# Signs of the weights from GpSimd, and two instructions instead of three for a weight block on VectorE

## The chip, the cores and the metric

The kernel runs on one core of one Trainium2 chip. The metric is device time in microseconds (us). The engines of the core are TensorE (PE; its weight loads are listed as PEld), VectorE (DVE), ScalarE (ACT), GpSimd (POOL) and SyncE (SP), which issues most of the DMAs. Each engine takes its instructions in the order in which they were written and waits on semaphores for the others.

## The reference

```python
q_n, k_n = rmsnorm(q, g_q), rmsnorm(k, g_k)         # q, k, v: 8 x 12 heads x 448 x 64, float32
attn = softmax(q_n @ k_n.T / sqrt(64))              # per head
x = (attn @ v) as 3584 tokens x 768
h = maximum(maximum(x @ w1, x @ w2), x @ w3)        # four weights of 768 x 768
out = h @ w_out                                     # float32, 3584 x 768
```

The four weights come out of the setup as 64-bit floats, two 32-bit words each. [...]

## The kernel before

**The order of the work.** The 96 heads are taken as 48 pairs, and each pair has 12 beats (`beat(g, i)`, pair g, beat i from 0). A beat issues a fixed list of pieces on all engines; `later(n, work)` puts work n beats on, and `tick()` at the end of a beat issues what is due. Nothing is reordered: the program's order is each engine's order. In a pair, VectorE takes the row maxima of the scores (L702) in beats 2, 5, 8 and 11, ScalarE the exponentials (L718), PE scores, transposes and products with V. At the same time the rows of Q and K of a later pair are prepared: GpSimd squares them (`sq`, L450, behind the row maxima of beats 2 and 5), VectorE sums the squares (`ss`, L457, beats 4 and 7), GpSimd makes the inverse root (`ri`, L467 and L471) and scales the rows (`kn`, `qn`, L479). In the first six pairs (`PLAIN = 6`) attention is done in 32-bit floats; from the seventh on everything is split into two 16-bit parts, and PE also has the two layers of the feed-forward network between (L889, L951).

**Ties.** In the first six pairs `follow()` ties GpSimd to VectorE: VectorE sets one element of `here` (L164), and GpSimd copies it (L165) and so waits until VectorE has come to that place. Before the change the ties lie ahead of the four row maxima of a pair, so that GpSimd's `sq`, `kn` and `qn` run beside them.

**The weights.** There are 24 blocks of 128 x 768 weights: 18 of w1, w2 and w3, then 6 of w_out. A block is loaded by SP into one of three `raw` buffers (768 KB, low and high words alternating, L224 and L229). The first 18 blocks are begun every 4 beats, the rest every 8 (`BLOCK_BEATS`). `prep_block` issues for each: on ScalarE a multiplication of the high words by 2 ** -112, in place (`rebias`, L189), and on VectorE three steps (`decode`), in the second, third and fourth beat after:

```python
f  = upper << 3                        # L197, tensor_scalar
f |= upper & 0x80000000                # L201, scalar_tensor_tensor
f |= lower >> 29                       # L206, scalar_tensor_tensor
```

Here `f` is the block's plain 32-bit form in the tile `w_sb`. The shift by 3 drops the sign bit, which the second step puts back. One beat later the buffer is loaded again. When three blocks are there, PE makes products of them (`marks`, L281), VectorE takes their largest (L169, `most`), GpSimd makes a scale (`w_up`, L300 and L301), and a block is split into two 16-bit parts, on ScalarE (L310) and VectorE (L313), two 128 x 768 operations. `largest_v` finds the largest value of V for a batch, by products on PE (L593) and a maximum on VectorE (L169, `v_rows`), in the later batches by VectorE alone.

Of the kernel before, what the change touches and what calls it, by code (L numbers as in the profile page):

```python
# [9 lines left out]
F32 = mybir.dt.float32  # L10
# [4 lines left out]
ALU = mybir.AluOpType  # L15
# [20 lines left out]
BLOCK_BEATS = (4, 8)  # L36
# [12 lines left out]
def qknorm_attention_maxout_ffn_kernel(  # L49
# [73 lines left out]
    def later(beats, work, last=False):  # L123

        due.setdefault(clock[0] + beats, ([], []))[last].append(work)
# [65 lines left out]
    def decode(raw, f, stage):  # L191

        bits = raw.rearrange("p (n t) -> p n t", t=2)
        upper, lower = bits[:, :, 1], bits[:, :, 0]
        f = f.bitcast(U32)
        if stage == 0:
            nc.vector.tensor_scalar(  # L197
                out=f, in0=upper, scalar1=3, scalar2=None, op0=ALU.logical_shift_left
            )
        elif stage == 1:  # L200
            nc.vector.scalar_tensor_tensor(  # L201
                out=f, in0=upper, scalar=0x80000000, in1=f,
                op0=ALU.bitwise_and, op1=ALU.bitwise_or,
            )
        else:
            nc.vector.scalar_tensor_tensor(  # L206
                out=f, in0=lower, scalar=29, in1=f,
                op0=ALU.logical_shift_right, op1=ALU.bitwise_or,
            )

    blocks = [("in", ft, j) for ft in range(NFT) for j in range(NJ)]
    blocks += [("out", ft, 3) for ft in range(NFT)]
# [22 lines left out]
    def prep_block(n):  # L235
        kind, ft, j = blocks[n]
        raw = raws[n]
        f = plain(w_sb, n) if kind == "in" else plain(wo_sb, ft)
        rebias(raw)

        for stage in range(3):
            later(2 + stage, lambda stage=stage: decode(raw, f, stage), True)
        if kind == "out":
            bound_block(ft, f)
        later(5 if kind == "in" else 9, load_raw)
        if j == NJ - 1:
            later(5, lambda: bound_in(ft), True)
        elif kind == "out" and ft == NFT - 1:
            later(10, bound_out, True)
# [317 lines left out]
    def largest_v(t):  # L567

        b, n = divmod(t, 2)
        if b not in v_rows:  # L570
            v_rows[b] = sb.tile([P, 2], F32, name="v_rows", bufs=2)
        rows = slice(0, P if b else KEYS)
        values = v_tiles[t][rows].rearrange("p h n d -> p (h n d)")
        to = v_rows[b]
        if b >= SQUARED:
            parts = sb.tile([P, 2], F32, name="v_parts", bufs=2)
            half = NP * 2 * D

            def second():
                row_largest(parts[:, 1:2], values[:, half:])  # L580
                nc.vector.tensor_tensor(
                    out=to[:, n:n + 1], in0=parts[:, 0:1], in1=parts[:, 1:2], op=ALU.max
                )

            row_largest(parts[:, 0:1], values[:, :half])
            later(2, second)
            return
        box = ps_m.tile([P, 512], F32, name="marks", tag="m")
        halves = values.bitcast(BF16).rearrange("p (n t) -> p n t", t=2)
        blocks = NP * 4 * D // P  # L590
        for c in range(blocks):
            f = halves[:, c * P:(c + 1) * P, 1]
            nc.tensor.matmul(box[:, 0:P], f, f, start=c == 0, stop=c == blocks - 1)  # L593
        later(1, lambda: row_largest(to[:, n:n + 1], box[:, 0:P]))
# [400 lines left out]

    x_of = [[] for _ in range(B)]
    queue = []
    decoded = [0]

    owed = [0.0]  # L1000

# [92 lines left out]
    def beat(g, i):  # L1094
        w, n = g - 1, g + 2
        c, part = divmod(i, 3)
        k = 4 * g + c
        early = k + 1 <= 4 * PLAIN
        if i == 0 and 0 < g <= PLAIN:
            keep_turned(w, 3)  # L1100
        if part == 0:
            if g < G:
                if k > 4 * PLAIN:
                    row_max(g, c)
                softmax(g, c)
            if early:
                scores(*divmod(k + 1, 4))
            if g < PLAIN:
                if c > 0:
                    turn_plain(g, c - 1)  # L1110
            elif k == 4 * PLAIN:
                pass
            elif 0 < k <= 4 * G:
                lower_weights(*divmod(k - 1, 4))
        if part == 1:
            if c > 0 and g < PLAIN:
                keep_turned(g, c - 1)
            if PLAIN <= g < G:
                upper_weights(g, c)
        if part == 2:  # L1120
            if early:
                if g < PLAIN:
                    follow()
                row_max(*divmod(k + 1, 4))
            elif k + 1 < 4 * G:
                scores(*divmod(k + 1, 4))
        if 0 <= w < PLAIN:
            if i == 1:
                guard_sums(w)
            if i == 2:  # L1130
                inverse_sums(w)
            if i == 5:
                spread_sums(w)
            if i == 6:
                keep_sums(w)
            if i == (8 if w < PLAIN else 9):
                scale_plain(w)
        if w >= 0 and i == (2 if w < PLAIN else 7):
            add_values(w)
        of = THIRDS if g > 2 * NP or (g == 2 * NP and i > 10) else THIRDS_0  # L1140
        thirds(of[i] + (len(queue) > 1 and i % 6 == 4))
        if w >= 0 and i == (9 if 0 < w < PLAIN else 10):
            finish(w, x_of[w // NP])
        if w >= 0 and g % NP == 0 and i == (6 if w < PLAIN else 10):
            queue.append(ffn(w // NP, x_of[w // NP]))

        if g + 1 < G:
            if g + 1 < PLAIN:
                if i in (1, 4):
                    turn_whole(g + 1, "kq"[i // 4])  # L1150
                if i in (2, 5):
                    keep_whole(g + 1, "kq"[i // 5])
            else:
                if i == 0:
                    upper_rows(g + 1, "q")
                if i in (0, 1):
                    lower_rows(g + 1, "kq"[i])
                if i in (2, 3):
                    turn_rows(g + 1, "kq"[i - 2])
                if i == 5:  # L1160
                    swap_keys(g + 1)

        if PLAIN <= n < G and i == 11:
            upper_rows(n, "k")
        if g < PLAIN:
            if i in (2, 5):
                squares(n, "kq"[i // 3])
            if i == 11:
                turn_plain(g, 3)
            if i in (4, 7):  # L1170
                sum_squares(n, "kq"[i // 7])
            if i in (5, 8):
                if i == 8:
                    scale_rows(n, "k")
                inv_rms(n, "kq"[i // 8])
            if i == (9 if n >= PLAIN else 11):
                scale_rows(n, "q")
        elif n < G:
            if i in (0, 3):
                squares(n, "kq"[i // 3])  # L1180
            if i in (2, 5):
                sum_squares(n, "kq"[i // 3])
            if i in (5, 7):
                inv_rms(n, "kq"[i // 7])
            if i in (8, 9):
                scale_rows(n, "kq"[i - 8])

        if g == 0 and i in (0, 3):
            load_v(i // 3)
            later(10 if i == 0 else 11, lambda: largest_v(i // 3))  # L1190
        if g % 3 == 0 and g + 6 < G and i == 9:
            load_v(g // 3 + 2)
            later(8, lambda: largest_v(g // 3 + 2))
        if g == 1 and i == 4:
            bound_v(0)
        if g % NP == NP - 1 and g + 1 < G and i == 7:
            bound_v(g // NP + 1)
        if PLAIN <= g < G and i == 9:
            scale_v(g)
        if PLAIN <= g < G and i == 11:  # L1200
            upper_v(g)
        if PLAIN <= w and i == 0:
            lower_v(w)
        if PLAIN <= w and i == 1:
            shift_values(w)

        if g + 3 < G:
            if i == 0:
                load_k(g + 3)
            if i == 1:  # L1210
                load_q(g + 3)
        if i == 2 and w >= PLAIN:
            turn_weights(w, 3)
        if PLAIN <= g < G and i in (5, 8, 11):
            turn_weights(g, i // 3 - 1)
        n_in = min(decoded[0], NFT * NJ)
        due_at = BLOCK_BEATS[0] * n_in + BLOCK_BEATS[1] * (decoded[0] - n_in)
        if decoded[0] < len(blocks) and clock[0] > due_at:
            later(0, lambda n=decoded[0]: prep_block(n), True)
            decoded[0] += 1  # L1220
        tick()
# [41 lines left out]
```

## Time and profile before

| | |
|---|---|
| Median of 3 runs | 1017.15 us (1016.62 to 1017.98) |
| The profiled execution | 1017.41 us, span 1015.6 us |
| Busy share of the span | PE 96%, VectorE 68%, ScalarE 62%, GpSimd 59% |
| VectorE from 50 to 100 us | 49.70 of 50 us |
| VectorE from 400 to 500 us | 70.90 of 100 us |
| GpSimd from 50 to 100 us | 36.45 of 50 us |
| PE idle up to 250 us | 33 us of 250 |

The span is the time from the first to the last instruction of the profiled execution; the device time includes what lies around it. All rows of the profile come from that one execution. A timeline row gives the start and the length of an instruction in us, the engine, the line, the operation, what it writes and reads, and, in brackets, how long the engine stood idle ahead of it and what ended that. A row of a tile or a line gives the least, the median and the largest length in nanoseconds. An operation may be recorded as beginning a little before the one ahead of it has ended.

### The profile page before, as it was taken

How to read it: one execution, taken by the hardware profiler on the slowest of the kernel's cores; microseconds unless marked ns; L12 is line 12 of the kernel's file. 1: busy time of each engine (PE TensorE's matmuls, PEld its weight loads, DVE VectorE, ACT ScalarE, POOL GpSimd, SP SyncE). 2: the span in 40 equal slices, each digit the busy share in tenths (PEclk: the TensorE clock that was granted, in tenths of full speed). 3: DMA queues.
4: the chain of work that ended last, by engine and by line, in shares of the span. 5: the costliest groups of instructions: out<-in, count | busy, mean ns of one | idle time of the engine just before them, and what ended most of it. 6: DMA issues, size and time to landing. Idle time of an engine off the chain costs nothing.

```text
span 1015.6 us, 17562 instructions
## 1 busy us (share of the span) xinstructions
PE 977.4 (96%) x6045; PEld 527.5 (52%) x6045; DVE 692.9 (68%) x1365; ACT 624.7 (62%) x1419; POOL 602.4 (59%) x683
## 2 busy tenths in 40 slices
PE   8988689889999999999999999999999999999998
PEld 5555345445555555555555555555555555555554
DVE  6899988887767666685767666775767657660120
ACT  6798675667666765666666666657666766651111
POOL 6677875678566666666776666666667757310000
PEclk9999889999999999999999999999999999999999
DMA  9867798989999899998989999999989998751001
GB/s 241 226 174 188 197 179 177 186 149 163 209 165 179 165 204 183 186 166 172 204 155 184 174 206 166 190 159 190 197 162 182 176 186 139 146 92 55 1 1 63
DMA packets 519550, 165.95 MB, mean 163 GB/s; under 512 B 494436, under 2 KB 515236, under 8 KB 519460
## 3 DMA queue, kind: packets, MB, share of 16 engines
q1 hardware_dynamic: 456480, 148.83, 75.5%
q10 hardware_dynamic: 62980, 16.00, 8.6%
q8 instruction: 48, 0.79, 0.3%
q14 instruction: 42, 0.34, 0.1%
HBM read 53.28 MB, written 11.01 MB: 63 GB/s over the span
## 4 chain that ended last, share of the span: by engine, by line
PE 60%; DMA 1%; DVE 0%; ACT 0%; issue 0%; SPq 0%
PE acc L889 34%; PE acc L951 12%; PE av L860 6%; PE sc L680 6%; PE sc L687 1%; DMA pt<-pp 0%; DVE pp L815 0%; DMA out_dram<-osb 0%; ACT osb L960 0%; DVE nm L702 0%; ACT pp L805 0%; ACT qp L499 0%; PE most L604 0%; ACT ht L909 0%; SPq L834 0%
## 5 line engine op out<-in xcount | busy, mean ns | idle before, releaser
L889 PE MATMUL acc<-xt,w_sb 128*128 128x448 f16 x2592 | 516.4, 354 | 0.0
L889 PEld LDWEIGHTS <-w_sb 128*128 128x128 f16 x2592 | 251.4, 98 | 242.3 <-issue 14.0
L718 ACT ACTIVATE sc<-sc,nm 128x448 f32<-128x448 f32 x294 | 178.9, 609 | 187.5 <-DVE nm L702 182.9
L702 DVE TENSOR_REDUCE nm<-sc 128x2 f32<-128x896 f32 x192 | 186.2, 970 | 99.4 <-PE sc L680 58.5
L805 ACT ACTIVATE pp<-sc,rs 128x448 f16<-128x448 f32 x294 | 173.0, 633 | 80.3 <-ACT sc L718 36.4
L815 DVE SCALAR_TENSOR_TENSOR pp<-sc,rs,pp 128x448 f16<-128x448 f32 x294 | 187.9, 675 | 0.9 <-ACT pp L805 0.9
L471 POOL TENSOR_TENSOR ri<-ri,half_neg 128x7 f32<-128x7 f32 x96 | 146.6, 1527 | 8.0
L951 PE MATMUL acc<-w_sb,ht 128*128 128x384 f16 x864 | 148.1, 326 | 1.6 <-ACT osb L960 1.3
L505 POOL TENSOR_TENSOR kp<-kn,kp 128x448 f16<-128x448 f32 x42 | 43.5, 1036 | 157.9 <-ACT kp L499 142.3
L680 PE MATMUL sc<-kt,qt 128*128 128x448 f16 x504 | 116.8, 354 | 10.6 <-DVE pp L815 10.4
L951 PEld LDWEIGHTS <-ht 128*128 128x128 f16 x864 | 83.7, 98 | 61.0 <-issue 5.8
L680 PEld LDWEIGHTS <-qt 128*128 128x128 f16 x504 | 48.8, 98 | 56.4 <-DVE pp L815 10.7
L860 PE MATMUL av<-pt,vp 128*64 128x448 f16 x672 | 72.6, 355 | 0.6 <-DMA pt<-pp 0.6
L918 POOL COPY hx<-ht 128x128 f16<-128x128 f16 x48 | 15.4, 322 | 95.6 <-DVE ht L913 94.9
L875 DVE SCALAR_TENSOR_TENSOR xt<-av,xt 128x448 f16<-128x448 f32 x42 | 26.2, 624 | 62.6 <-ACT xt L874 62.6
L647 POOL TENSOR_TENSOR vp<-vr,vp 128x512 f16<-128x512 f32 x42 | 49.3, 1174 | 21.0 <-ACT vp L641 21.0
L457 DVE TENSOR_REDUCE ss<-sq 128x7 f32<-128x448 f32 x96 | 57.9, 603 | 5.1 <-ACT sq L448 4.3
L505 POOL TENSOR_TENSOR qp<-qn,qp 128x448 f16<-128x448 f32 x42 | 46.3, 1103 | 22.3 <-ACT qp L499 21.4
L903 DVE TENSOR_TENSOR m<-acc,m 128x448 f32<-128x448 f32 x54 | 33.1, 614 | 33.1 <-PE acc L889 33.0
L860 PEld LDWEIGHTS <-vp 128*64 128x64 f16 x672 | 36.0, 109 | 34.7 <-issue 15.8
L488 POOL TENSOR_TENSOR qn<-qn,gain 128x448 f32<-128x448 f32 x42 | 49.0, 1167 | 3.3
L467 POOL TENSOR_SCALAR ri<-ss 128x7 f32<-128x7 f32 x54 | 20.1, 373 | 51.1 <-DVE ss L457 49.9
(140 smaller groups left out, 1159.2 us busy)
## 6 DMA issues: line engine op xcount, KB each, us to landing
raw<-in_moe_w_dram SPq DMA_DIRECT2D x18, 768.0 KB, 5.6
kt<-kt SPq DMA_DIRECT2D x84, 112.0 KB, 2.6
out_dram<-osb SPq DMA_DIRECT2D x24, 384.0 KB, 2.6
vr<-in_v_dram SPq DMA_DIRECT2D x42, 192.0 KB, 4.2
kr<-in_k_dram ACTq DMA_DIRECT2D x34, 224.0 KB, 3.1
qr<-in_q_dram ACTq DMA_DIRECT2D x34, 224.0 KB, 4.4
raw<-in_moe_w_out_dram SPq DMA_DIRECT2D x6, 768.0 KB, 5.0
vs<-vp SPq DMA_DIRECT2D x84, 48.0 KB, 2.5
```

The costliest lines, as they stand in the source:

```text
L457: nc.vector.tensor_reduce(sums[g % 2][:, KQ[what]], sq, axis=AX, op=ALU.add)
L471: nc.gpsimd.tensor_tensor(out=ri, in0=ri, in1=half_neg[:, at], op=ALU.pow)
L505: nc.gpsimd.tensor_tensor(out=parts[:, :, 1], in0=n, in1=parts[:, :, 0], op=ALU.subtract)
L647: nc.gpsimd.tensor_tensor(out=vp[:, 1], in0=values_of(g).rearrange("p h n d -> p (h n) d"), in1=vp[:, 0], op=ALU.subtract,)
L680: nc.tensor.matmul(sc[:, h, :S], qt[:, 4 * h + c], kt[:, n, keys[h]], start=n == 0, stop=n == 1,)
L702: nc.vector.tensor_reduce(nm[:, :n], sc[:, :n, :S], axis=AX, op=ALU.max, negate=True)
L718: nc.scalar.activation(to, sc[:, h, :S], AF.Exp, bias=nm[:, h:h + 1], accum_out=total,)
L805: nc.scalar.activation(pp[:, h, 0], sc[:, h, :S], AF.Copy, scale=rs[:, h:h + 1])
L815: nc.vector.scalar_tensor_tensor(out=pp[:, h, 1], in0=sc[:, h, :S], scalar=rs[:, h:h + 1], in1=pp[:, h, 0], op0=ALU.mult, op1=ALU.subtract,)
L860: nc.tensor.matmul(av[half, :S], values, pt[:, 7 * h + block, SHIFT[h]:SHIFT[h] + S], start=n == 0, stop=n == len(steps) - 1,)
L889: nc.tensor.matmul(acc[:, :S], wt[:, wp, c], xs[c][:, xp], start=(c == 0 and n == 0), stop=(c == NCT - 1 and n == 2),)
L951: nc.tensor.matmul(acc[:, :HW], lhs, wo_sb[:, f, wp, half * HW:(half + 1) * HW], start=(f == 0 and n == 0), stop=(f == NFT - 1 and n == 2),)
```

## The change

GpSimd multiplies the high words of a block, read as 32-bit floats, by 0.0: the result is a zero with the weight's sign, and it is written to the block's place in `w_sb` (the new `sign`). VectorE then needs two steps: `f |= upper << 3`, in one instruction with two inputs, and `f |= lower >> 29`. They come in the second and third beat after `rebias`, and the raw buffer of the first 18 blocks is loaded again one beat earlier. `sign` must read the high words before `rebias` changes them, so it is issued 3, 1 or 2 beats ahead of the block's beginning for the three blocks of a pair (beats 10, 4 and 7), and 2 ahead for w_out. In the first six pairs each `sign` has a tie of its own ahead of it. `largest_v` comes 11 beats after the load of V, not 8.

```diff
         if stage == 0:
-            nc.vector.tensor_scalar(
-                out=f, in0=upper, scalar1=3, scalar2=None, op0=ALU.logical_shift_left
-            )
-        elif stage == 1:
             nc.vector.scalar_tensor_tensor(
-                out=f, in0=upper, scalar=0x80000000, in1=f,
-                op0=ALU.bitwise_and, op1=ALU.bitwise_or,
+                out=f, in0=upper, scalar=3, in1=f,
+                op0=ALU.logical_shift_left, op1=ALU.bitwise_or,
             )
...
+    def sign(n):
+
+        kind, ft, j = blocks[n]
+        f = plain(w_sb, n) if kind == "in" else plain(wo_sb, ft)
+        nc.gpsimd.tensor_scalar(
+            out=f, in0=raws[n].bitcast(F32).rearrange("p (n t) -> p n t", t=2)[:, :, 1],
+            scalar1=0.0, scalar2=1.0, op0=ALU.mult, op1=ALU.mult,
+        )
...
-        for stage in range(3):
+        for stage in range(2):
             later(2 + stage, lambda stage=stage: decode(raw, f, stage), True)
...
-        later(5 if kind == "in" else 9, load_raw)
+        later(4 if kind == "in" else 9, load_raw)
...
+        m = signed[0]
+        ahead = 2 if m >= NFT * NJ else (3, 1, 2)[m % 3]
+        if m < len(blocks) and clock[0] > due_at(m) - ahead:
+            if g < PLAIN:
+                follow()
+            sign(m)
+            signed[0] += 1
...
-            later(8, lambda: largest_v(g // 3 + 2))
+            later(11, lambda: largest_v(g // 3 + 2))
```

GpSimd in the fourth pair before, from the tie of beat 8 to the scaling of Q's rows (the numbers at the names are those of the buffers):

```order
L165 COPY seen_131<-here_1002 1x1
L479 TENSOR_TENSOR kn_1015<-kr_667,ri_971 128x448
L467 TENSOR_SCALAR ri_971<-ss1_130 128x7
L471 TENSOR_TENSOR ri_971<-ri_971,half_neg_84 128x7
L165 COPY seen_131<-here_1047 1x1
L479 TENSOR_TENSOR qn_1067<-qr_678,ri_971 128x448
```

And in the same place now, from the tie of beat 7; `w_sb<-raw` is `sign`, and the lines of the program are 5 further down:

```order
L165 COPY seen_131<-here_1034 1x1
L211 TENSOR_SCALAR w_sb_132<-raw_912 128x768
L165 COPY seen_131<-here_1040 1x1
L484 TENSOR_TENSOR kn_1046<-kr_690,ri_1006 128x448
L472 TENSOR_SCALAR ri_1006<-ss1_130 128x7
L476 TENSOR_TENSOR ri_1006<-ri_1006,half_neg_84 128x7
L165 COPY seen_131<-here_1082 1x1
L211 TENSOR_SCALAR w_sb_132<-raw_1009 128x768
L165 COPY seen_131<-here_1088 1x1
L484 TENSOR_TENSOR qn_1098<-qr_701,ri_1006 128x448
```

One `sign` with its tie stands ahead of K's scaling, another ahead of Q's. The pair's third (beat 4) stands between the squares of K and of Q.

VectorE in the fourth pair before, from the reciprocal of beat 2 to Q's sum of squares in beat 7:

```order
L765 RECIPROCAL sum_660<-sum_660 128x7
L197 TENSOR_SCALAR w_sb_132<-raw_795 128x768
L457 TENSOR_REDUCE ss1_130<-sq_899 128x7
L201 SCALAR_TENSOR_TENSOR w_sb_132<-raw_795,w_sb_132 128x768
L313 SCALAR_TENSOR_TENSOR w_sb_132<-w_sb_132,w_up_135 128x768
L164 MEMSET here_953 1x1
L702 TENSOR_REDUCE nm_956<-sc_908 128x2
L206 SCALAR_TENSOR_TENSOR w_sb_132<-raw_795,w_sb_132 128x768
L169 TENSOR_REDUCE most_903<-marks_932 128x1
L457 TENSOR_REDUCE ss1_130<-sq_969 128x7
```

And now:

```order
L770 RECIPROCAL sum_683<-sum_683 128x7
L197 SCALAR_TENSOR_TENSOR w_sb_132<-raw_801,w_sb_132 128x768
L164 MEMSET here_956 1x1
L462 TENSOR_REDUCE ss1_130<-sq_932 128x7
L202 SCALAR_TENSOR_TENSOR w_sb_132<-raw_801,w_sb_132 128x768
L318 SCALAR_TENSOR_TENSOR w_sb_132<-w_sb_132,w_up_135 128x768
L164 MEMSET here_988 1x1
L707 TENSOR_REDUCE nm_991<-sc_939 128x2
L169 TENSOR_REDUCE most_934<-marks_967 128x1
L164 MEMSET here_1034 1x1
L462 TENSOR_REDUCE ss1_130<-sq_1004 128x7
```

Each sum of squares now has a tie ahead of it, and the block is done before the row maximum of beat 5, where a third step stood behind that maximum. On SP two raw loads, in the fifth and sixth pairs, now stand ahead of the transposing DMA of K instead of behind it; PE's products for V's largest (L593) stand three beats later.

More of the change, by code (lines that the diff above doesn't have):

```diff
@@ L997, in qknorm_attention_maxout_ffn_kernel, with due_at @@
     queue = []
-    decoded = [0]
+    decoded, signed = [0], [0]
+    def due_at(n):
+        n_in = min(n, NFT * NJ)
+        return BLOCK_BEATS[0] * n_in + BLOCK_BEATS[1] * (n - n_in)
     owed = [0.0]
@@ L1215, in beat @@
             turn_weights(g, i // 3 - 1)
-        n_in = min(decoded[0], NFT * NJ)
-        due_at = BLOCK_BEATS[0] * n_in + BLOCK_BEATS[1] * (decoded[0] - n_in)
-        if decoded[0] < len(blocks) and clock[0] > due_at:
+        if decoded[0] < len(blocks) and clock[0] > due_at(decoded[0]):
             later(0, lambda n=decoded[0]: prep_block(n), True)
```

## The prediction

> **What bounds the kernel now.** The page's first part was read first:
> ```profile
> PE 977.4 (96%) x6045; PEld 527.5 (52%) x6045; DVE 692.9 (68%) x1365; ACT 624.7 (62%) x1419; POOL 602.4 (59%) x683
> ```
> TensorE is busy 96% of the span, but that is a mean over stages, so the busy time by stretch was read next: one whole head pair (the fourth, from its row maximum in beat 2 to the next pair's), the pair after it, and a late stretch. Columns: stretch, length, then PE, PEld, DVE, ACT, POOL busy with instruction counts, granted clock, DMA share, GB/s.
> ```profile
> 64.05:80.34 16.29, 14.97 (x118) 8.48 (x116) 16.22 (x29) 14.77 (x34) 10.70 (x14) 1.00 0.84 200
> 80.34:98.44 18.10, 16.61 (x127) 9.88 (x123) 17.94 (x29) 16.01 (x35) 14.55 (x17) 1.00 0.68 189
> 400.00:500.00 100.00, 100.00 (x618) 53.67 (x616) 70.90 (x147) 64.81 (x151) 65.94 (x75) 1.00 0.96 179
> ```
> Late in the run PE is full, and no edit touches its work; what is won or lost early moves the end by as much. In the fourth pair VectorE is busy 16.22 of 16.29 us and sets the pace, PE could give up at most 16.29 - 14.97 = 1.3 us, and GpSimd has 5 us free. In the fifth GpSimd is at 14.55 of 18.10. So the question is what VectorE gains there, and whether GpSimd, which gets the work, still keeps up.
>
> The timeline of the fourth pair, VectorE:
> ```profile
> 65.16 0.54 DVE L197 TENSOR_SCALAR w_sb<-raw 128x768 uint32<-128x768 uint32 x1
> 65.62 0.61 DVE L457 TENSOR_REDUCE ss<-sq 128x7 f32<-128x448 f32 x1
> 66.15 0.94 DVE L201 SCALAR_TENSOR_TENSOR w_sb<-raw,w_sb 128x768 uint32<-128x768 uint32 x1
> 67.02 1.00 DVE L313 SCALAR_TENSOR_TENSOR w_sb<-w_sb,w_up 128x768 f16<-128x768 f32 x1
> 67.95 1.08 DVE L702 TENSOR_REDUCE nm<-sc 128x2 f32<-128x896 f32 x1
> 72.25 1.30 DVE L313 SCALAR_TENSOR_TENSOR w_sb<-w_sb,w_up 128x768 f16<-128x768 f32 x1
> 73.48 0.95 DVE L201 SCALAR_TENSOR_TENSOR w_sb<-raw,w_sb 128x768 uint32<-128x768 uint32 x1
> ```
> And GpSimd; the bracket is idle time ahead of a row:
> ```profile
> 64.36 0.92 POOL L450 TENSOR_TENSOR sq<-kr 128x448 f32<-128x448 f32 x1
> 68.18 0.17 POOL L165 COPY seen<-here 1x1 f32<-1x1 f32 x1 [2.90 <-DVE here L164]
> 69.32 0.80 POOL L467 TENSOR_SCALAR ri<-ss 128x7 f32<-128x7 f32 x1
> 71.81 0.93 POOL L479 TENSOR_TENSOR kn<-kr,ri 128x448 f32<-128x448 f32 x1
> 72.82 0.80 POOL L467 TENSOR_SCALAR ri<-ss 128x7 f32<-128x7 f32 x1
> 73.71 2.06 POOL L471 TENSOR_TENSOR ri<-ri,half_neg 128x7 f32<-128x7 f32 x1
> 76.10 0.18 POOL L165 COPY seen<-here 1x1 f32<-1x1 f32 x1 [0.33 <-DVE here L164]
> 78.09 0.48 POOL L301 TENSOR_SCALAR w_up<-w_up 128x1 f32<-128x1 f32 x1
> 80.48 0.17 POOL L165 COPY seen<-here 1x1 f32<-1x1 f32 x1 [1.91 <-DVE here L164]
> 80.62 0.92 POOL L450 TENSOR_TENSOR sq<-kr 128x448 f32<-128x448 f32 x1
> ```
> Three things are to be seen. GpSimd's idle time lies in front of its ties: 2.90 + 0.33 + 1.91 = 5.14 us. From the copy at 68.18 to L301's end at 78.57 it runs 10.39 us with only 0.33 us free. And K's squares end at 64.36 + 0.92 = 65.28, just 0.34 us ahead of the sum that needs them at 65.62: if GpSimd is late in beat 2, VectorE waits.
>
> The two engines also get in each other's way:
> ```profile
> 23.52 0.93 POOL L479 TENSOR_TENSOR kn<-kr,ri 128x448 f32<-128x448 f32 x1
> 23.54 1.72 DVE L206 SCALAR_TENSOR_TENSOR w_sb<-raw,w_sb 128x768 uint32<-128x768 uint32 x1
> L197 DVE TENSOR_SCALAR w_sb<-raw x24: 522/550/1417, 17.1 to 192.8; 128x768 uint32<-128x768 uint32 x24
> L206 DVE SCALAR_TENSOR_TENSOR w_sb<-raw,w_sb x24: 939/970/1829, 20.0 to 197.1; 128x768 uint32<-128x768 uint32 x24
> L467 POOL TENSOR_SCALAR ri<-ss x54: 210/211/901, 5.3 to 863.8; 128x7 f32<-128x7 f32 x54
> L467 POOL TENSOR_SCALAR ri<-ss,k_mean,k_eps x42: 354/367/1048, 85.5 to 860.8; 128x7 f32<-128x7 f32 x42
> L471 POOL TENSOR_TENSOR ri<-ri,half_neg x96: 1480/1490/2308, 5.6 to 864.0; 128x7 f32<-128x7 f32 x96
> L633 POOL TENSOR_SCALAR vr<-vr,v_up x42: 679/690/1389, 129.8 to 898.2; 128x512 f32<-128x512 f32 x42
> ```
> L206, 0.97 us in the median, took 1.72 us beside kn. The other way round, L467 took 0.80 us at 72.82, while L313 ran, where 0.211 us is its median.
>
> **The change part by part.** The sum is made against the profiled execution's 1017.41 us (its span is 1015.6), 0.26 us above the median of the runs, 1017.15.
>
> *Removed: 24 times L197.* It is the cheapest of the three: in VectorE's stream it holds 65.62 - 65.16 = 0.46 us, so a pair with three blocks is shorter by 1.4 us if nothing else happens. The new first instruction has two SBUF inputs like L201, and is priced like it.
>
> *Added: 24 sign instructions on GpSimd.* No row has this form. From 7 to 512 elements the one-input form with per-partition scalars goes from 0.367 to 0.690 us, 0.64 ns an element; constants instead of such scalars save 0.367 - 0.211 = 0.156. For 768 elements: 0.690 + 256 x 0.00064 - 0.156 = 0.70 us. The upper end is the two-input rate, 0.93/448 x 768 = 1.6 us. I take 0.75, near the first, since it is one input, with a little for the stride of two words. With its tie's copy (0.17) and two gaps of 0.05 a sign costs GpSimd 1.02 us in pairs 1 to 6. The Trainium skill (GPSIMD Engine Reference, Performance pitfalls for Q7 kernels) adds half to reads whose step is over 8 bytes; this step is 8, and no run here shows either side. By that surcharge an estimate would be 1.1 us a sign and 0.7 us more for two of them in a pair.
>
> *What that does to a pair.* One sign (beat 4) falls into the 2.90 us idle before 68.18. Two (beats 7 and 10) fall into the chain that has 10.39 us of rows: 10.39 + 2 x 1.02 = 12.43. The loop in which GpSimd is never idle is then:
> - from the end of K's squares: the sum of squares, 0.53 (66.15 - 65.62), and beside it the tie (68.18 - 67.95 = 0.23), the copy (80.62 - 80.48 = 0.14) and the sign, which lets VectorE in about 0.2 before its recorded end: 0.23 + 0.14 + 0.75 - 0.2 = 0.92; then the second assembly 0.87 (67.02 - 66.15), L313 0.93, the next tie 0.23: 2.95, against 68.18 - 65.28 = 2.90 now;
> - the chain, 12.43;
> - copy, gap and K's squares, 81.54 - 80.48 = 1.06, and 0.1 between.
>
> That is 2.95 + 12.43 + 1.06 + 0.1 = 16.54 us against 16.26 now (80.62 - 64.36): +0.3 a pair, although VectorE has less to do. The 0.2 before the end is from L313 at 72.25: 1.30 us is 0.30 over its other row's 1.00, while kn (to 72.74) ran 0.49 us into it. The Trainium skill (SBUF — State Buffer, Who interferes with whom) has the pair of ports locked for the whole instruction. By that rule VectorE would get in at 1.12, and a pair would cost 0.2 more. The row says less.
>
> *Waits at the shared port on top.* The present chain holds some already: 0.80 - 0.21 twice and 2.06 - 1.49, 1.75 us in all. The first goes, because L206 no longer lies behind the row maximum of beat 5. New ones come, since kn, the sign of beat 10 and qn now start a sign later, into VectorE's back-to-back runs (L313 with an assembly; assembly, L313, assembly). Ends: -1.75, if all such waits vanish, and +1.9 for two more whole instructions of 0.95. I take +0.7, nearer the upper end, because every late operation meets such a run. So +1.0 a pair, between -1.3 (PE's limit) and +2.2; four full pairs (third to sixth) give +4.0, from -5.2 to +8.8.
>
> *The first two pairs.*
> ```profile
> 15.36 0.89 ACT L189 ACTIVATE raw<-raw 128x768 f32<-128x768 f32 x1
> 15.57 0.56 POOL L1054 TENSOR_TENSOR even<-even,root 128x1 f32<-128x1 f32 x1
> 31.12 0.29 DVE L169 TENSOR_REDUCE v_rows<-marks 128x1 f32<-128x128 f32 x1 [0.45 <-PE marks L593]
> 34.62 0.94 ACT L189 ACTIVATE raw<-raw 128x768 f32<-128x768 f32 x1 [0.30 <-DMA raw<-in_moe_w_dram]
> 36.68 0.29 DVE L169 TENSOR_REDUCE v_rows<-marks 128x1 f32<-128x128 f32 x1 [1.11 <-PE marks L593]
> ```
> The sign must read the raw block before L189 rewrites it, so ScalarE now waits for GpSimd, with the exponentials queued behind and PE's transposes waiting for those; each new tie holds GpSimd's squares or kn behind it in the same way. Block 0's sign can start only after L1054 (16.13), so its L189 goes from 15.36 to about 17.1: 1.7 us. Block 4's must wait for the load that L189 waited for at 34.62, with Q's squares behind it. Against that, largest_v three beats later takes away VectorE's 0.45 and 1.11 us of waiting, and the L197 of these blocks fall away too. GpSimd has no w_up work yet. I take -1.5, between -3 and +1.7.
>
> *Blocks 18 to 23, the loads, the rest.* After the sixth pair the ties are gone, blocks come every eight beats, and 0.46 us saved stands against a sign of 0.75 us each: 0, within 1 us. A raw load is issued a beat earlier; twice it passes K's transpose on the SP queue, which then waits behind it for VectorE's second assembly; within that 1 us. The one-element memsets cost VectorE's stream nothing that shows.
>
> Sum: 4.0 - 1.5 + 0 = +2.5, so 1019.9 as profiled, 1019.7 as a median.
>
> **The rivals.**
> *GpSimd has room, VectorE's saving stays (faster).* For: 5.14 us idle a pair against 3 x 1.02; the three waits at the port could shrink as the runs get shorter. Against: the idle time does not lie where the two late signs go. It decides if GpSimd still idles before the copy of beat 2. At 0.8 us a pair over six pairs, -5: about 1012; at PE's limit, -8: 1009.
> *Runs of VectorE starve GpSimd (slower still).* Each pair +2.2: 8.8 - 1.5, about 1024.5.
> *A wash.* Waits at the port come out even, +0.3 a pair: 1.2 - 1.5, 1017.
>
> **How the numbers follow.** Forecast 0.40, of which 0.12 lies below 1019.2; faster rival 0.32; starved 0.12; wash 0.16. A measurement tells 0.2%, 2 us, from no change. So faster 0.32; within 0.2%: 0.12 + 0.16 = 0.28; slower 0.28 + 0.12 = 0.40. The range leaves out the faster rival's lower part (0.1) and the end of the starved case (0.05): 1011.5 to 1025.
>
> **What would show it.** Right: in pairs 4 to 6 the copy of beat 2 starts without idle time, the sum of K's squares waits for GpSimd's squares, pairs last 17 us or more, POOL is the busiest engine there. Wrong: the fourth pair under 16 us with VectorE still at 99%, a sign over 1 us or under 0.6, or VectorE waiting for ScalarE's L189 in each block.

## The result and the profile after

| | before | after |
|---|---|---|
| Median of 6 runs each, same chip | 1017.57 us (1016.23 to 1019.23) | 1022.84 us (1021.70 to 1024.08) |
| Ratio to before, 95% interval | | 1.0054 (1.0041 to 1.0067) |
| Profiled execution, span | 1017.41, 1015.6 us | 1023.35, 1021.6 us |
| Third pair begins (row maximum of its beat 2) | 47.43 us | 49.12 us |
| Pairs 3 to 5, up to the sixth pair's row maximum | 51.01 us | 54.70 us |
| First product with the weights (`acc`) | 128.30 us | 136.93 us |

The kernel became slower by 5.3 us. Of the 6.0 us in the span, 1.7 are there when the third pair begins, 3.7 come in pairs 3 to 5, and 3.2 up to the first `acc`; the sum there is 8.6, and 2.6 are won back later. The sixth pair, from its row maximum to the seventh's, is the largest loss of a single pair: 20.31 us before (98.44 to 118.75), 24.42 after (103.82 to 128.24).

The first part of the page after:
```profile
PE 980.8 (96%) x6045; PEld 528.7 (52%) x6045; DVE 691.2 (68%) x1360; ACT 625.4 (61%) x1419; POOL 626.6 (61%) x726
```
GpSimd has 24.2 us more work (it was 602.4). VectorE has 24 instructions of about half a microsecond less, and yet its busy time fell by 1.7 us only. Where the rest went is seen in the groups of VectorE's weight work in pairs 3 to 5, first of before:
```profile
L206 DVE SCALAR_TENSOR_TENSOR w_sb<-raw,w_sb 128x768 uint32<-128x768 uint32 x10 | 11.3, 1127 | 0.2
L313 DVE SCALAR_TENSOR_TENSOR w_sb<-w_sb,w_up 128x768 f16<-128x768 f32 x9 | 9.7, 1081 | 0.0
L201 DVE SCALAR_TENSOR_TENSOR w_sb<-raw,w_sb 128x768 uint32<-128x768 uint32 x9 | 8.5, 945 | 0.0
L197 DVE TENSOR_SCALAR w_sb<-raw 128x768 uint32<-128x768 uint32 x9 | 5.8, 648 | 0.0
```
and of after, with the row of the windows for that stretch:
```profile
L202 DVE SCALAR_TENSOR_TENSOR w_sb<-raw,w_sb 128x768 uint32<-128x768 uint32 x10 | 15.6, 1556 | 0.0
L318 DVE SCALAR_TENSOR_TENSOR w_sb<-w_sb,w_up 128x768 f16<-128x768 f32 x9 | 14.2, 1574 | 0.0
L197 DVE SCALAR_TENSOR_TENSOR w_sb<-raw,w_sb 128x768 uint32<-128x768 uint32 x9 | 9.7, 1080 | 0.0
49.12:103.82 54.70, 48.59 (x347) 27.35 (x344) 54.57 (x83) 45.84 (x100) 44.66 (x61) 0.94 0.63 174
```
28 instructions took 39.5 us where 37 took 35.3. No work was added to them: the mean of the last step of the assembly went from 1.13 to 1.56 us and that of the split from 1.08 to 1.57. VectorE (the third busy time in the row) is never idle, 54.57 of 54.70 us. What the prediction calls waiting at the shared port is inside an instruction's recorded length here, so a view of idle time and releasers shows nothing of it. Below, such a lengthening is called a hold.

The fourth pair after shows who holds it (these are the rows that matter, not all). VectorE:
```profile
69.92 1.54 DVE L202 SCALAR_TENSOR_TENSOR w_sb<-raw,w_sb 128x768 uint32<-128x768 uint32 x1
77.24 1.83 DVE L202 SCALAR_TENSOR_TENSOR w_sb<-raw,w_sb 128x768 uint32<-128x768 uint32 x1
81.53 2.80 DVE L318 SCALAR_TENSOR_TENSOR w_sb<-w_sb,w_up 128x768 f16<-128x768 f32 x1
84.26 0.94 DVE L202 SCALAR_TENSOR_TENSOR w_sb<-raw,w_sb 128x768 uint32<-128x768 uint32 x1
```
GpSimd:
```profile
69.76 0.88 POOL L211 TENSOR_SCALAR w_sb<-raw 128x768 f32<-128x768 f32 x1
75.59 0.91 POOL L211 TENSOR_SCALAR w_sb<-raw 128x768 f32<-128x768 f32 x1
76.45 0.90 POOL L165 COPY seen<-here 1x1 f32<-1x1 f32 x1
77.32 0.93 POOL L484 TENSOR_TENSOR kn<-kr,ri 128x448 f32<-128x448 f32 x1
80.67 0.99 POOL L165 COPY seen<-here 1x1 f32<-1x1 f32 x1
81.63 0.86 POOL L211 TENSOR_SCALAR w_sb<-raw 128x768 f32<-128x768 f32 x1
82.59 0.93 POOL L484 TENSOR_TENSOR qn<-qr,ri 128x448 f32<-128x448 f32 x1
83.49 1.26 POOL L305 TENSOR_TENSOR w_up<-most,half_neg 128x1 f32<-128x1 f32 x1
84.84 0.42 POOL L306 TENSOR_SCALAR w_up<-w_up 128x1 f32<-128x1 f32 x1
85.29 0.17 POOL L165 COPY seen<-here 1x1 f32<-1x1 f32 x1
```
An undisturbed L202 is the last VectorE row, 0.94 us. The sign at 69.76 held the first one for 0.6 us, kn at 77.32 the second for 0.9, and the sign at 81.63 with qn behind it held the split (L318) for 1.8 (2.80 against 1.00, its other length in this pair): 3.3 us in a pair that saves three times 0.46. Each engine has to wait for the other in turn (the one-element copies at 76.45 and 80.67 took 0.90 and 0.99 us instead of 0.17), and the copy at 85.29 follows without a gap.

### The profile page after: what moved, and what is told of

Read it like the earlier page. It is cut to its first block, busy times and chain, and to the rows that moved or that the text cites. A ratio compares the mean times of both kernels' runs of the same rounds, so it can differ in the third digit from the quotient of the medians.

```text
span 1021.6 us, 17636 instructions
## 1 busy us (share of the span) xinstructions
PE 980.8 (96%) x6045; PEld 528.7 (52%) x6045; DVE 691.2 (68%) x1360; ACT 625.4 (61%) x1419; POOL 626.6 (61%) x726
## 5 line engine op out<-in xcount | busy, mean ns | idle before, releaser
L476 POOL TENSOR_TENSOR ri<-ri,half_neg 128x7 f32<-128x7 f32 x96 | 143.9, 1499 | 8.0
L493 POOL TENSOR_TENSOR qn<-qn,gain 128x448 f32<-128x448 f32 x42 | 51.4, 1225 | 3.3
L914 ACT ACTIVATE ht<-acc 128x448 f16<-128x448 f32 x42 | 22.9, 546 | 41.7 <-DVE acc L908 41.7
```

Of the source, the lines that this page charges most:

```text
L476: nc.gpsimd.tensor_tensor(out=ri, in0=ri, in1=half_neg[:, at], op=ALU.pow)
L493: nc.gpsimd.tensor_tensor(out=n, in0=n, in1=gain.rearrange("p (o d) -> p o d", o=1).broadcast_to([P, UNITS, D]), op=ALU.mult,)
```

## The experiments

The theory: VectorE's saving is real, but the two late signs of a pair push kn, the next sign and qn into VectorE's runs of instructions with two SBUF inputs, and the holds at the shared port, counted as VectorE's work, cost more than the saving. (SBUF is the memory in which tiles such as `raw` and `w_sb` lie.) The rivals: the saving is worth nothing; GpSimd's time alone is the cost, whatever its instructions touch; the new ties are; the first two pairs are, where ScalarE's L189 waits for the sign. The times in the table are those of the runs; the two columns on pairs are from each kernel's one profile (start of the third pair, length of pairs 3 to 5, between VectorE's row maxima). The ratio is to the kernel before, run beside it (1016.08 to 1016.56 us there, 1017.57 beside after). How far a single profile can be trusted is seen in v_later, last_six and beat4_from6, which are alike up to the third pair: it begins at 45.78 to 46.43 us, so differences under 0.7 us say nothing there. Pairs 3 to 5 are alike in v_later and last_six and differ by 0.04. All kernels but before have `largest_v` at its later beat.

| Kernel | Median us | Ratio (95%) | Pair 3 begins | Pairs 3 to 5 |
|---|---|---|---|---|
| before | | 1 | 47.43 | 51.01 |
| after | 1022.84 | 1.0054 (1.0041 to 1.0067) | 49.12 | 54.70 |
| no_sign | 1008.34 | 0.9922 (0.9908 to 0.9937) | 45.92 | 46.48 |
| both_ways | 1030.10 | 1.0134 (1.0118 to 1.0151) | 50.40 | 58.61 |
| pow_for_sign | 1013.31 | 0.9969 (0.9958 to 0.9980) | 47.17 | 49.92 |
| zeros_only | 1015.93 | 0.9992 (0.9981 to 1.0003) | 48.69 | 50.02 |
| no_tie | 1019.62 | 1.0029 (1.0018 to 1.0040) | 48.85 | 53.36 |
| from_block6 | 1020.65 | 1.0037 (1.0025 to 1.0050) | 46.45 | 53.89 |
| v_later | 1014.70 | 0.9982 (0.9971 to 0.9992) | 46.43 | 50.97 |
| last_six | 1014.36 | 0.9980 (0.9971 to 0.9989) | 45.78 | 51.01 |
| beat4_only | 1016.17 | 0.9994 (0.9985 to 1.0002) | 47.36 | 50.72 |
| beat4_no_tie | 1013.01 | 0.9965 (0.9953 to 0.9978) | 46.44 | 49.87 |
| two_no_tie | 1016.02 | 1.0004 (0.9992 to 1.0015) | 47.28 | 50.28 |
| beat4_from6 | 1011.73 | 0.9953 (0.9939 to 0.9967) | 46.39 | 49.47 |

**The saving alone (no_sign).**
```diff
-                out=f, in0=upper, scalar=3, in1=f,
+                out=f.rearrange("p (a n) -> p a n", n=P),
+                in0=upper.rearrange("p (a n) -> p a n", n=P), scalar=3,
+                in1=zeros.unsqueeze(1).broadcast_to([P, NCT, P]),
...
-            if g < PLAIN:
-                follow()
-            sign(m)
```


> The changed kernel without the 24 sign instructions and their copies: VectorE's first step ORs the shifted words with a constant tile of zeros, so the weights lose their signs; VectorE still takes two steps a block, each with two SBUF inputs. Theory (VectorE is held at the shared port by GpSimd's sign and by kn and qn, which it delays): with the sign gone the saving of 0.46 us a block comes through, pairs 3 to 6 last about 15.5 us where PE allows it, pair 2 is no longer than before; 1008 to 1013 us. Rival (the saving is worthless, PE, ScalarE or GpSimd's old chain set the pair): within 2 us of the kernel before, 1016 to 1019.

Measured: 1008.34 us, 7.9 below the kernel before by the ratio. The later bound of the values is in this, 1.8 us by v_later below; the other 6 are for the two steps, and they lie within the 5 to 8 that the prediction's faster rival gave the change, if GpSimd isn't charged for it. The weight groups of VectorE in pairs 3 to 5:
```profile
L200 DVE SCALAR_TENSOR_TENSOR w_sb<-raw,zeros 128x768 uint32<-128x768 uint32 x9 | 10.3, 1141 | 0.0
L207 DVE SCALAR_TENSOR_TENSOR w_sb<-raw,w_sb 128x768 uint32<-128x768 uint32 x10 | 9.5, 948 | 0.0
L323 DVE SCALAR_TENSOR_TENSOR w_sb<-w_sb,w_up 128x768 f16<-128x768 f32 x9 | 9.3, 1028 | 0.0
```
The same 28 instructions take 29.1 us; after, they take 39.5. The difference, 10.4 us in three pairs, is what the signs and the lateness that they give GpSimd's other work cost them: 3.5 us a pair, near the 3.3 read from the fourth.

**The cost alone (both_ways).** The sign is issued as in the changed kernel, and VectorE's old three steps follow and overwrite it (`shift` and `own_sign` are the old first and second step, `decode(raw, f, 1)` is the last). The raw buffer is loaded again one beat later, as in the kernel before.
```diff
-            for stage in range(2):
-                later(2 + stage, lambda stage=stage: decode(raw, f, stage), True)
-            later(4 if kind == "in" else 9, load_raw)
+            later(2, lambda: shift(raw, f), True)
+            later(3, lambda: own_sign(raw, f), True)
+            later(4, lambda: decode(raw, f, 1), True)
+            later(5 if kind == "in" else 9, load_raw)
```


> The changed kernel in which GpSimd makes the signed zeros as there, but VectorE then assembles the block in its three old steps and overwrites them: GpSimd's cost without VectorE's saving. Theory (holds at the port are VectorE's time): the saving of 1.4 us a pair is lost on top, so 4 to 8 us over the changed kernel, 1027 to 1031. Rival (GpSimd's own never idle loop sets the pair and hides VectorE's work): within 2 us of the changed kernel, 1021 to 1025.

Measured: 1030.1 us, the theory's. Pairs 3 to 5 are 58.61 - 54.70 = 3.91 us longer than after, 0.43 a block: the price of L197 in the prediction (0.46) was right, and GpSimd's loop hides almost none of it.

**GpSimd's time without the data (pow_for_sign).**
```diff
+            if g < PLAIN:
+                follow()
+            nc.gpsimd.tensor_tensor(
+                out=aside, in0=root[:, 0:2], in1=half_neg[:, 0:2], op=ALU.pow
+            )
```
added to no_sign.

> The kernel without signs (first step ORs with a constant zero, 1008.3 us) with GpSimd's time put back without the data: in each sign's place its tie and a power of 128 x 2 numbers, some 0.6 to 0.9 us by the rows of the other powers, whose reads and writes are tiny. Theory (both the sign's own hold on VectorE and the lateness that it gives kn and qn cost): the sign's own holds, about 1.5 of the 3.5 us a pair, vanish, the others stay: 1012 to 1017. Rival A (GpSimd's time alone is the cost): 1019 to 1022, as the changed kernel. Rival B (only the data that the sign reads and writes costs): 1008 to 1011.

Measured: 1013.31 us. The power took 0.79 us in the mean, a sign 0.95 after, so GpSimd's time was put back a little short. Of the 1.0054 - 0.9922 = 1.3% that the signs cost, time on GpSimd with the ties is 0.9969 - 0.9922 = 0.5%; the larger part, 0.85%, needs the data. In pairs 3 to 5 it is 49.92 - 46.48 = 3.4 us of the 8.2 between no_sign and after. For pairs 3 to 5 both rivals fall, and the theory stands: kn and qn come later and hold VectorE, and the sign itself holds it on top, 1.6 us a pair (the theory had 1.5). How little the power itself does is seen here, GpSimd first:
```profile
66.09 0.70 POOL L1168 TENSOR_TENSOR aside<-root,half_neg 128x2 f32<-128x2 f32 x1
```
and VectorE beside it:
```profile
66.26 0.94 DVE L209 SCALAR_TENSOR_TENSOR w_sb<-raw,w_sb 128x768 uint32<-128x768 uint32 x1
77.49 1.83 DVE L325 SCALAR_TENSOR_TENSOR w_sb<-w_sb,w_up 128x768 f16<-128x768 f32 x1
```
L209 runs at its 0.94 us. The split at 77.49 is held by qn, which came at 77.57: one operation of 0.9 us where after had two.

In the sixth pair it is otherwise, and rival A is right: with the power it lasts 24.20 us (97.09 to 121.29), with the sign 24.42, with neither 21.17 (no_sign, 92.40 to 113.57). There VectorE waits for GpSimd's squares of K, with no data in the sign's place:
```profile
102.18 0.62 DVE L469 TENSOR_REDUCE ss<-sq 128x7 f32<-128x448 f32 x1 [3.08 <-POOL sq L462]
```
So the change pays twice: for holds in pairs 3 to 5 and for GpSimd's time in the sixth.

**Writing without reading (zeros_only).**
```diff
-        nc.gpsimd.tensor_scalar(
-            out=f, in0=raws[n].bitcast(F32).rearrange("p (n t) -> p n t", t=2)[:, :, 1],
-            scalar1=0.0, scalar2=1.0, op0=ALU.mult, op1=ALU.mult,
-        )
+        nc.gpsimd.memset(f, 0.0)
```


> The changed kernel with GpSimd writing plain zeros in the sign's place (a memset of 128 x 768 that reads no SBUF, about 0.7 us by its row of 128 x 128), ties kept, so the weights lose their signs. Theory (the hold is at the SBUF ports, and a write takes them as well): VectorE's assembly beside the memset is held as beside the sign, 1018 to 1022. Rival (only reading holds VectorE): as with the power in the sign's place, 1012 to 1015.

Measured: 1015.93 us, between the two ranges, so the time decides nothing. The rows do. GpSimd:
```profile
78.61 0.73 POOL L211 MEMSET w_sb<- 128x768 f32 x1
79.55 0.93 POOL L481 TENSOR_TENSOR qn<-qr,ri 128x448 f32<-128x448 f32 x1
```
VectorE:
```profile
78.54 1.01 DVE L315 SCALAR_TENSOR_TENSOR w_sb<-w_sb,w_up 128x768 f16<-128x768 f32 x1
79.47 1.83 DVE L202 SCALAR_TENSOR_TENSOR w_sb<-raw,w_sb 128x768 uint32<-128x768 uint32 x1
```
A write of 128 x 768 inside L315's 1.01 us costs neither engine anything (the 24 memsets took 0.73 to 0.74 us each); qn, which reads, holds the next instruction for 0.9. So the theory's second half, that a write holds too, was wrong, and the rival is right about the mechanism: pairs 3 to 5 took 50.02 us, as with the power (49.92). The Trainium skill (SBUF — State Buffer, Who interferes with whom) says as much: with two SBUF inputs a VectorE instruction contends with a GpSimd instruction that reads SBUF, not with one that only writes it. The run agrees. What keeps the time above the rival's range is the first two pairs, 48.69 - 47.17 = 1.5 us longer than with the power; why was not found.

**The ties (no_tie).**
```diff
-            if g < PLAIN:
-                follow()
             sign(m)
```


> The changed kernel without the memset and copy that tie each of the first 18 signs to VectorE. Theory (the holds come from the sign and what it delays): the signs and the holds stay, GpSimd is 0.2 to 0.3 us a sign shorter: 1020 to 1024. Rival (the ties are the cost, since GpSimd's squares and kn stand behind them): the loss goes, 1015 to 1018.

Measured: 1019.62 us, just under the theory's range and over the rival's. By the ratios the ties cost 0.25%, 2.5 of the 5.5 us; the prediction had counted little beyond 0.22 us of GpSimd's time for each. Pairs 3 to 5 are 1.3 us shorter, and it is the split that gained, 2.8 us (14.2 in the changed kernel), while the two steps of the assembly lost 1.5 (26.8 against 25.3):
```profile
L318 DVE SCALAR_TENSOR_TENSOR w_sb<-w_sb,w_up 128x768 f16<-128x768 f32 x9 | 11.4, 1264 | 0.0
```
A tie lets GpSimd go at a moment that VectorE's place sets, and in beat 4 that is while VectorE sums, just ahead of its assembly; what that costs is taken up below.

**The first two pairs (from_block6, v_later, last_six).** from_block6 leaves blocks 0 to 5 in three steps:
```diff
+    def by_sign(n):
+        return n >= 6
...
-            if g < PLAIN:
-                follow()
-            sign(m)
+            if by_sign(m):
+                if g < PLAIN:
+                    follow()
+                sign(m)
```


> The changed kernel with the blocks of the first two pairs (0 to 5) in three steps and without sign; 6 to 23 as changed. Theory (pair 2 lost 2.1 us to ScalarE's rewrite, which waits for the sign, and to ties): 2 to 3 us under the changed kernel, which stood 5.3 over the kernel before: 1018 to 1020. Rival (the prediction's term: the change gains 1.5 us in the first two pairs, which is now lost): 1022 to 1024.

Measured: 1020.65 us, 1.7 us under the changed kernel by the ratios (the intervals overlap), a little above the theory's range and below the rival's. In the profile the third pair begins 2.7 us earlier. So by the profile the signs lose in the first two pairs, and do not gain. v_later is the kernel before with later values' bounds alone (`return False`, no signs), last_six has signs for blocks 18 to 23 besides (`return n >= 18`).

> The kernel before with one edit of the change alone: the bounds of the values (largest_v) three beats later; all blocks in three steps, no signs. With signs for the last six blocks besides, it took 1014.4, and its pair 2 was 16.55 us where the kernel before has 17.95. Theory (the later bound takes VectorE's waits of 0.45 and 1.11 us away in pair 2, and the last six signs bring nothing): 1014 to 1015.5. Rival (the last six signs bring the gain): 1016 to 1017.

> Signs on GpSimd for blocks 18 to 23 alone; the first 18 in three steps, without sign or tie (largest_v stays at its later beat). Theory (after the sixth pair PE is full, and neither the saving nor the sign counts): within 2 us of the kernel before, 1015 to 1018.5. Rival (blocks 18 to 23 carry part of the loss, as GpSimd's busy time of 23.2 of 25 us at 125 to 150 us suggests): 1019 to 1021.

Measured: 1014.70 (in its theory's range) and 1014.36 us. last_six came out under its theory's range because the later bound, which that range had left out, gives 0.18% by itself: the third pair begins 1.0 us earlier than before. The six last signs bring nothing that can be told. What happens to the start is seen in ScalarE's rewrite of block 0 and VectorE's maximum of V after:
```profile
16.93 0.90 ACT L189 ACTIVATE raw<-raw 128x768 f32<-128x768 f32 x1 [1.80 <-POOL w_sb L211]
33.68 0.29 DVE L169 TENSOR_REDUCE v_rows<-marks 128x1 f32<-128x128 f32 x1 [3.45 <-PE marks L598]
```
and in v_later:
```profile
31.51 0.29 DVE L169 TENSOR_REDUCE v_rows<-marks 128x1 f32<-128x128 f32 x1 [0.86 <-PE marks L621]
```
With the signs ScalarE stands idle for 1.8 us, and VectorE waits for the products of V 3.45 us instead of 0.86. That the one makes the other is not shown, and zeros_only speaks against it. Its memset doesn't read the raw block, so L189 doesn't wait for it, and VectorE waits for the products nearly as long:
```profile
14.97 0.89 ACT L189 ACTIVATE raw<-raw 128x768 f32<-128x768 f32 x1
34.05 0.29 DVE L169 TENSOR_REDUCE v_rows<-marks 128x1 f32<-128x128 f32 x1 [2.46 <-PE marks L595]
```
The third pair begins at 48.69 us there, only 0.4 before the changed kernel's, and at 48.85 without ties. Of the 2.7 us that the signs lose in the first two pairs (49.12 against 46.43 in v_later), the power with its ties makes 0.7, the write 1.5 more, and what the reading adds, L189's wait with it, 0.4; only the 1.5 is clear of the 0.7 by which alike kernels differ. Which wait carries the loss stays open.

**Fewer signs (beat4_only, beat4_no_tie, two_no_tie, beat4_from6).** Signs in beat 4 only, `return n % 3 == 1 or n >= 18`; the same without the tie; those of beats 4 and 7 without ties, `n % 3 != 0 or n >= 18`; and beat 4 from block 6 on without ties, `n >= 18 or (n >= 6 and n % 3 == 1)`.

> The sign on GpSimd only for the block of a pair whose sign comes in beat 4, where GpSimd had 2.9 us idle, and for the last six; the two others of a pair in three steps as before. Theory (it is the two late signs that push kn, the next sign and qn into VectorE's runs): those holds go, one block in three saves 0.46 us, and its sign costs VectorE 0.6: about as before, 1015 to 1019. Rival (the work is too much for GpSimd wherever it stands, or the first pairs' wait for the sign costs it): the loss shrinks only by the share of signs, to 1019 to 1021.

> The kernel with one sign a pair (beat 4) and in the last six blocks, without the tie. Theory (a tie costs because GpSimd's squares and kn stand behind it, and it cost 2 us over 18 signs): with six of them 0.5 to 1 us is gained, 1015 to 1016. Rival (without its tie the sign starts earlier, beside VectorE's first assembly, and holds that): no gain or a loss, 1016 to 1018.

> Two signs a pair, those of beats 4 and 7, without ties, and in the last six blocks; the block whose sign would come in beat 10 in three steps. Theory (each late sign delays kn into VectorE's run, a hold of about 0.9 us against 0.46 saved): the second sign costs 0.4 us a pair over the kernel with beat 4 alone (1013.0), 1013.5 to 1017. Rival (without the tie the sign of beat 7 lies beside VectorE's row maximum and its step on PSUM, and only that of beat 10 hurts): 1009 to 1012.5.

> As the kernel with one sign a pair in beat 4 without tie (1013.0), but the six blocks of the first two pairs in three steps without sign. Theory (in the first two pairs a sign gains nothing, since ScalarE's rewrite waits for it: pair 2 was 17.67 with it and 16.55 without): 1011 to 1013. Rival (VectorE's saving counts there too): 1013.5 to 1015.

Measured: 1016.17, 1013.01, 1016.02 and 1011.73 us; the second lies under both of its ranges (its ties had cost more than either allowed), the others in their theories'. The kernel to compare with is v_later (0.9982), which has the later bound and no signs. One sign a pair with its tie is no gain: it saves 0.46 and costs 0.6. The tie decides. In beat4_only, GpSimd:
```profile
65.90 0.88 POOL L229 TENSOR_SCALAR w_sb<-raw 128x768 f32<-128x768 f32 x1
```
VectorE:
```profile
66.06 1.54 DVE L220 SCALAR_TENSOR_TENSOR w_sb<-raw,w_sb 128x768 uint32<-128x768 uint32 x1
```
In beat4_from6, GpSimd:
```profile
63.76 1.24 POOL L229 TENSOR_SCALAR w_sb<-raw 128x768 f32<-128x768 f32 x1
```
VectorE:
```profile
63.67 0.54 DVE L212 TENSOR_SCALAR w_sb<-raw 128x768 uint32<-128x768 uint32 x1
64.13 0.61 DVE L485 TENSOR_REDUCE ss<-sq 128x7 f32<-128x448 f32 x1
64.66 1.16 DVE L220 SCALAR_TENSOR_TENSOR w_sb<-raw,w_sb 128x768 uint32<-128x768 uint32 x1
```
Without the tie the sign starts right behind K's squares, waits itself for L212, has the port while VectorE sums, and holds L220 for 0.2 us instead of 0.6. A second sign a pair (two_no_tie) costs 0.4% by the end, in the theory's range, but 0.4 us in pairs 3 to 5 together, where the theory had 0.4 in each; the sixth pair is 1.2 us longer (23.94 against 22.71). Leaving the first two pairs alone gives the best kernel here, 1011.73 us, 0.47% under the kernel before, 0.3% under v_later and 1.0% under the changed one, by the ratios.

## Why the prediction was right, point by point

- *Slower, by GpSimd's late signs and the port:* shown for pairs 3 to 5. no_sign and both_ways bracket it: the saving is worth some 6 us and the later bound 1.8, the signs with their ties cost 13 (1.0054 - 0.9922). In the sixth pair the cost is GpSimd's time, port or not (pow_for_sign).
- *The third to the sixth pair, +1.0 us each:* pairs 3 to 5 came out +1.7, +1.4 and +0.6, 1.2 in the mean, and the sixth +4.1: 7.8 us in place of 4.0. Inside the term the parts were off. The sign took 0.884 us in the median, not 0.75. The waits that were to bring +0.7 a pair came to +3.0 in pairs 3 to 5: above their shortest lengths (0.54 to 1.00 us, by the rows) VectorE's weight instructions took 12.7 us after and 3.6 before, an estimate, while L197's 1.4 a pair fall away. The view of the loop ("GpSimd never idle") fits: the copy of beat 2 at 85.29 follows L306 without a gap. But VectorE is never idle either, and putting its L197 back costs nearly in full (both_ways); that the two loops are one, tied together at the port, is argued from this.
- *K's sum of squares would wait for GpSimd's squares in pairs 4 to 6:* not in 4 and 5, where VectorE came to the sum after the squares. It does in the sixth and again ahead of the seventh pair's row maximum:
```profile
108.47 0.62 DVE L462 TENSOR_REDUCE ss<-sq 128x7 f32<-128x448 f32 x1 [1.93 <-POOL sq L455]
127.70 0.62 DVE L462 TENSOR_REDUCE ss<-sq 128x7 f32<-128x448 f32 x1 [2.01 <-POOL sq L455]
```
  These two waits, which were 0 and 0.72 us before, make most of the sixth pair's +4.1, where the prediction had +1.0. There GpSimd is the bound:
```profile
100.00:125.00 25.00, 18.76 (x113) 11.83 (x109) 22.16 (x34) 17.30 (x40) 22.54 (x28) 0.86 0.65 172
125.00:150.00 25.00, 18.62 (x110) 9.98 (x109) 21.15 (x39) 16.08 (x35) 23.20 (x24) 0.86 0.84 187
```
  GpSimd (the fifth busy time) is at 22.54 and 23.20 of 25 us, VectorE at 22.16 and 21.15. "POOL is the busiest engine" holds here, not in the fourth pair.
- *The first two pairs, -1.5 us:* the step that failed. They came out +1.7. Of its parts the later values' bound came as forecast in kind (-1.0 in v_later, for two waits of 0.45 and 1.11). L189 of block 0 begins at 16.93, near the forecast 17.1, but the saving that was to outweigh such waits does not show: the signs lose 2.7 us there (49.12 against 46.43). L189's wait can hardly be the main cause, since most of the loss stays in zeros_only without it; the cause is open.
- *Blocks 18 to 23, 0 within 1 us:* right for the signs (last_six against v_later, -0.3 us with intervals that overlap). Besides, of the 8.6 us lost at the first `acc` 2.6 came back, which the prediction had not foreseen; in the windows from 139 to 250 us PE is busy for 103.05 us after and 100.00 before. That it catches up because more of its work is ready is argued, not shown.
- *The sum, +2.5:* that it came as near to the measured +5.3 as it did is partly luck. When the seventh pair begins, the loss is 9.5 us (128.24 against 118.75), where the terms up to there gave 2.5; 3.5 of it came back by the end, for which the prediction had no term.
- *The surcharge for the step:* the Trainium skill (GPSIMD Engine Reference, Performance pitfalls for Q7 kernels) adds half beyond 8 bytes, and the sign, at 8, does not pay it: its median is far from the 1.1 us that the prediction had worked out for that case.
```profile
L211 POOL TENSOR_SCALAR w_sb<-raw x24: 864/884/1708, 16.0 to 191.1; 128x768 f32<-128x768 f32 x24
```
- *The port given free some 0.2 us before GpSimd's recorded end:* 0.1 to 0.2. L202 at 69.92 needs 0.94 and ended at 71.46, so it got in at 70.52, 0.12 ahead of the sign's 70.64; the split at 81.53 got in at 83.33, 0.19 ahead of qn's 83.52.

## What to carry to other kernels

Work moved from VectorE to GpSimd is not paid for by GpSimd's idle time, if it reads SBUF and VectorE's instructions beside it have two SBUF inputs: ask beside which VectorE instruction each GpSimd operation will lie, and which others it pushes along. Then look stage by stage for one in which GpSimd itself has no room, as in the sixth pair here. A wait at the shared port counts as busy time, so look for instructions of one form whose lengths spread (here 0.94 to 1.83 us), not for idle time. Where a tie lets GpSimd go just as VectorE turns to instructions with two SBUF inputs, dropping it or putting the work beside a sum may keep the gain: against v_later, one sign a pair so placed from the third pair on was worth 0.3% (beat4_from6, 0.9953 against 0.9982), and three with their ties cost 0.7% (after).

## What the runs showed of the hardware that had not been expected

- GpSimd's plain write of 128 x 768 (0.73 us) ran inside a VectorE instruction with two SBUF inputs (1.01 us), and neither was longer.
- A power of 128 x 2 numbers (0.70 us) doesn't hold VectorE's two-input instruction beside it (0.94 us), though it reads SBUF. The Trainium skill (SBUF — State Buffer, Who interferes with whom) has the port pair locked for the whole instruction; this row does not fit that for the recorded length; that an operation which reads little and computes long holds the port for a small part of its time is how the row is read here, not shown by itself.
- In the fourth pair after, a waiting GpSimd operation went first where VectorE passed from one two-input instruction to the next (kn ahead of L202 at 77.24, the sign ahead of the split at 81.53), and the sign and qn, one behind the other, kept one split waiting for 1.8 us.
